# Twelve raw fp32 expert units: the first layer as three products of halves, the second layer left raw

## The chip, the cores and the metric

One NeuronCore of a Trainium2 chip runs the whole kernel. The metric is device time in microseconds (us) of one execution. Names of engines: PE is TensorE (PEld its weight loads), ACT is ScalarE, DVE is VectorE, POOL is GpSimd, SP is the queue that issues most transfers.

## The reference, cut to what matters

A gated linear recurrence runs over four sequences of 3648 tokens with 256 channels. Its output, 14592 rows of 256, goes through a two-level mixture of experts: the largest of 4 group logits and the largest of 4 expert logits inside that group pick one of 16 experts for each token, and that expert's two-layer network is scaled by the product of the two softmax weights.

```python
a_t  = exp(8 * sigmoid(r_gate) * log(sigmoid(a_param)))
h    = a_t[:, t] * h + sqrt(1 - a_t**2)[:, t] * sigmoid(i_gate)[:, t] * x[:, t]   # over t
...
g = argmax(y @ w_group);  e = argmax(y @ w_expert[g])          # per token
out = softmax weights * ( relu(y @ w1[g, e]) @ w2[g, e] )      # w1: 256 x 1024, w2: 1024 x 256
```

## The kernel before, in words

The tokens go through the recurrence in 16 chunks: chunk 0 has 4 blocks of 128 tokens, chunks 1 to 13 have 8, the last two have 4 and 2. For each chunk SP loads `a`, `i` and `x` (two halves each), ACT does the tanh, exp, square and sqrt passes, DVE the products and the scan (L374). PE then turns two blocks at a time into rows (`rows1`, L381, "rows" below) and ACT copies them out of PSUM (`rows2`, L387). DVE computes the routing, PE ranks the tokens (L463, L464), and POOL scatters the rows to lists, one list for each expert, in DRAM (`scatter`, L484, one indirect transfer for each block).

The expert work runs in units of 256 tokens of one expert. A unit takes its rows from the list (`gather`), turns them on PE (four transposes, L1006 for the raw units), and multiplies by `w1` in four steps j = 0 to 3 (first layer), each followed by a relu on ACT and by step j of the second layer with `w2`, one step behind. At the end ACT and DVE scale the two halves of the result (`finish`, L969 and L971) and POOL sends them to the output (`give`, L977).

There are three kinds of expert work, in this order on PE:

- Eight blocks of 128 tokens for four resident experts (`Block`, L1061 and L1073), whose raw fp32 weights lie in four places, k = 0 to 3. Each place is two tiles, one for `w1` and one for `w2`: `w1h0`,`w1l0` / `w2h0`,`w2l0` / `w1h1`,`w1l1` / `w2h1`,`w2l1`.
- Units 0 to 11 (`NATIVE = 12`), which multiply in raw fp32: `w1` is `m.w[0]`, `w2` is `m.w[1]`, the rows `m.x`. Unit u uses place u mod 4. These are `mm1_native` (L1016) and `mm2_native` (L1030).
- From unit 12 on, the units split weights, rows and relu results into two halves in `float32r` (a high half, and a low half that is the difference) and take three products, high by high, high by low, low by high (L886 and L951). Each unit uses all four tiles of b = u mod 2. Units from 26 on need the table that is made after the last chunk; the tail units (three blocks, L886 with 384 columns) end the kernel.

A planner (`Plan`) runs when the kernel is built. Every operation has an engine, an estimated cost, a due time, what it must follow and which buffers it takes, and the planner writes out one fixed order for each engine. Each engine executes its own order and waits where data or a buffer is not there. `STEPN` is the spacing of the due times of the twelve raw units. Buffers that matter here: one `q_o` (the second layer's result in PSUM), one `q_y` (rows, ranks, counts and the small row tables in PSUM), two `q_h` and two `hs` (before and after the relu), two `g` (gathered rows), three `o` (results on their way out).

The expert table of a stage comes from `counts` (L623), 24 small DVE operations and `in_row1` (L670); units 8 to 16 wait for the second such table.

Of the kernel before, what the change touches and what calls it, by code (L numbers as in the profile page):

```python
# [8 lines left out]
F32 = mybir.dt.float32  # L9
F32R = mybir.dt.float32r  # L10
# [35 lines left out]
class Plan:  # L46
# [14 lines left out]
    def op(self, engine, cost, emit, due, after=(), new=(), use=(), dma=0, table=None, soon=0.0, order=()):  # L61
        o = Op(engine, cost, emit, due, new, use, dma, table, soon)
        after = dict.fromkeys(a for a in after if a)
        order = dict.fromkeys(a for a in order if a and a not in after)
        o.wait = len(after) + len(order)
        for b in o.new + o.use:
            b.left += 1
        for a in after:
            a.then.append(o)
        for a in order:  # L70
            a.next.append(o)
        self.ops.append(o)
        return o
# [79 lines left out]
def rglru_moe_kernel(ctx: ExitStack, tc: tile.TileContext, x, r_gate, i_gate, a_param,  # L153
                     w_group, w_expert, w1, w2, out):
    nc = tc.nc
    V, S, G, T, DMA = nc.vector, nc.scalar, nc.gpsimd, nc.tensor, nc.sync

    P, NB = 128, 4
    D, NTOK = x.shape
    SEQ = NTOK // NB  # L160
    NT = NTOK // P
    NE = 16
# [14 lines left out]
    RES, RSTAGES = (0, 4, 8, 12), (1, 2)  # L177
    STAGES = [(4, 8), (7, 9), (10, 9)]
    NATIVE = 12

    BUFS = dict(i=4, x=4, a=8, v=4, wf=6, g=2, xs=2, hs=2, o=3, cl=4)
    PBUFS = dict(q_r=2, q_y=1, q_h=2, q_o=1)
# [11 lines left out]
    ROUTE = OROWS + 12  # L194
    AHEAD = 8

    STEP2, STEPB, STEPN = 10.5, 7.2, 14.5
    FIRST = range(1, 5)
    URGENT = (0, 1, 2, 3, 4, 7)
    ORES = 60  # L200
# [11 lines left out]
            rings[n] = Ring(k)  # L212
            pools[n] = ctx.enter_context(tc.tile_pool(name="p_" + n, bufs=k, **kw))
    rings["gb"] = Ring(NR)
    rings["raw"] = Ring(NR)
    for n in ("d", "oe", "bs", "pi"):
        rings[n] = Ring(2)

    def buf(n):
        return Buf(rings[n])  # L220
# [574 lines left out]
    class Unit:  # L795
        def __init__(self, u, tb, t, due):
            self.u, self.b, self.tb, self.t, self.due = u, u % 2, tb, t, due
            self.nb = 3 if tb is tT else 2
            self.hh, self.hl, self.qo, self.wf, self.cnd, self.c3 = {}, {}, [None] * 3, {}, {}, {}
            self.native = u < NATIVE and tb in tAs  # L800
            self.always = tb is tT or t < 2 or u < NATIVE + 2

        def col(self, what, h):
# [176 lines left out]
        tc.add_to_no_dep_group("out", ins.ins)  # L980


    def raw_places(k):
        b, half = divmod(k, 2)
        names = (("w1h", "w1l"), ("w2h", "w2l"))[half]
        return [wp.tile([P, 2, F] if half == 0 else [P, NF, D], F32, name=f"{n}{b}").rearrange("p a b -> p (a b)")
                for n in names]

    raw = [raw_places(k) for k in range(NR)]

# [4 lines left out]
    def load_native(m, i):  # L995
        if i == 0:
            m.w = raw_places(m.u % NR)
            e = m.reg("ei", [ENG.SP], NE - 1)
            m.src = [t_[bass.ds(e, 1)].rearrange("o p n -> (o p) n") for t_ in (w1, w2)]
        DMA.dma_start(m.w[i], m.src[i])  # L1000

    def turn_native(m):
        m.qx = pools["q_r"].tile([P, 512], F32, name="q_r")
# [83 lines left out]
    def add_blocks(s, ck, rows, masked, scattered):  # L1087
        bs = [Block(s, k, ck.due + ORES + k * STEPB) for k in range(NR)]
        for m in bs:
            due = m.due  # L1090
            bg, bx, q, bc = buf("gb"), buf("xs"), buf("q_r"), buf("cl")
            ga = op("SP", 0.1, lambda m=m: rows_block(m), ck.due + 20, [rows] + scattered, [bg], dma=P * DW * 4)
            tr = op("PE", 0.22, lambda m=m: turn_block(m), due - PREP, [ga], [q], [bg], order=trs[-1:])
            oc = op("DVE", 0.32, lambda m=m: cols_block(m), due - PREP, [tr, masked], [bc], [bg], order=ocs[-1:])
            ocs.append(oc)
            cp = op("ACT", 0.38, lambda m=m: copy_block(m), due - PREP, [tr], [bx], [q], order=cps[-1:])
            trs.append(tr)
            cps.append(cp)
            bo = buf("q_o")
            m1, rl, bh = [], [], []  # L1100
            for j in range(2):
                q = buf("q_h")
                m1.append(op("PE", 1.87, lambda m=m, j=j: mm1_block(m, j), due + j * 1.8, [cp, ld_raw[m.k][0]] + seq[-1:], [q], [bx, raw_b[m.k]]))
                seq.append(m1[-1])
                bh.append(buf("hs"))
                rl.append(op("ACT", 0.6, lambda m=m, j=j: relu_block(m, j), due + j * 1.8 - HASTE, [m1[j]], [bh[j]], [q]))
            for j in range(2):
                seq.append(op("PE", 1.82, lambda m=m, j=j: mm2_block(m, j), due + 3.5 + j * 1.8, [rl[j], ld_raw[m.k][1]] + seq[-1:],
                              [bo] if j == 0 else [], [bh[j], raw_b[m.k]] + ([bo] if j else [])))
            b = buf("o")  # L1110
            f_ = op("DVE", 0.48, lambda m=m: finish_block(m), due, seq[-1:] + [oc], [b], [bo, bc])
            op("POOL", 1.1, lambda m=m: give_block(m), due + STEPB, [f_], use=[b, bc], dma=P * D * 4)
# [12 lines left out]
    def add_native(m, before):  # L1125
        due = m.due
        early = due - WAHEAD
        B = 0.2155
        bw = buf("raw")
        ws = []  # L1130
        for i in range(2):
            ws.append(op("SP", 0.1, lambda i=i: load_native(m, i), early + i * 4, [m.tb.row], [bw] if i == 0 else [],
                         [bw] if i else [], dma=2 * P * F * 4, order=m.lw[-1:]))
            m.lw.append(ws[-1])
        bg, m.bc = buf("g"), buf("cl")
        ga = op("SP", 0.1, lambda: gather(m), early, [m.tb.row] + m.tb.scs, [bg], dma=2 * P * DW * 4, order=gas[-1:])
        gas.append(ga)
        bx, q = buf("xs"), buf("q_r")
        tr = op("PE", 0.107 * 4, lambda: turn_native(m), due - PREP, [ga] + trs[-1:], [q], [bg])
        trs.append(tr)  # L1140
        m.oc = op("DVE", 0.34, lambda: columns(m), due - PREP, [tr], [m.bc], [bg], order=ocs[-1:])
        ocs.append(m.oc)
        cp = op("ACT", 0.6, lambda: copy_native(m), due - PREP, [tr], [bx], [q], order=cps[-1:])
        cps.append(cp)

        def second(j):
            m.p2.append(op("PE", 8 * B, lambda j=j: mm2_native(m, j), due + (j + 1) * STEPN / J,
                           seq[-1:] + [rl[j], ws[1]], [bo] if j == 0 else [], [bh[j], bw] + ([bo] if j else [])))
            seq.append(m.p2[-1])
            if j == J - 1:  # L1150
                add_results(m, [bo], due + STEPN)
        m.p1, m.p2 = [], []
        pend = getattr(before, "pend", None)
        rl, qh, bh = [], {}, {}
        bo = buf("q_o")
        for j in range(J):
            q, bh[j] = buf("q_h"), buf("hs")

            def p1(j=j):
                qh[j] = mm1_native(m, j)  # L1160
            mm = op("PE", 8 * B, p1, due + j * STEPN / J, [cp, ws[0]] + seq[-1:], [q], [bx, bw])
            rl.append(op("ACT", 0.6, lambda j=j: relu_native(m, j, qh[j]), due + j * STEPN / J - HASTE, [mm], [bh[j]], [q]))
            m.p1.append(mm)
            seq.append(mm)
            if pend:
                pend()
            pend = lambda j=j: second(j)
        m.pend = pend
# [78 lines left out]
    def add_counts(gen, costs, due, after, n, more=False, ck=None):  # L1247
        q = buf("q_y")
        cn = op("PE", 0.1, counts, due, after, [q])
        if ck:  # L1250
# [4 lines left out]
    raw_b = [buf("raw") for _ in RES]  # L1255
    ld_raw = [[op("SP", 0.06, lambda k=k, i=i: load_raw(k, i), 40 + k * 9 + 4.5 * i, dma=2 * P * F * 4, soon=32 + k * 9,
                  new=raw_b[k:k + 1] if i == 0 else [], use=raw_b[k:k + 1] if i else []) for i in range(2)] for k in range(NR)]
    seq, gas, trs, cps, ocs = [], [], [], [], []
    ACTWF = []
    scs, eA, res = [], None, []  # L1260
# [24 lines left out]
    for u, m in enumerate(us):  # L1285
        m.lw = chain_lw
        m.lent = []
        if m.native:
            add_native(m, us[u - 1] if u else None)
            continue  # L1290
        if u < NATIVE + 2:
            m.lent = [o for n in us[:NATIVE] if n.u % NR // 2 == m.b for o in n.p1 + n.p2]
        add_unit(m, us[u - 1] if u else None, us[u - 2] if u > 1 else None)
    m.pend()
    cks[0].routed.wait += 1
# [73 lines left out]
```

## Time and profile before

| | us |
|---|---|
| median of 3 runs (range) | 928.49 (927.67 to 932.93) |
| profiled execution, its own time | 938.17 |
| its span in the trace | 936.4 |
| PE busy in the span | 854.5 (91%) |
| first raw unit's first product | 151.27 |
| first product of unit 12 | 376.5 |

The profile's rows give a line of the kernel, the engine, the operation, and what it writes and reads. A raw fp32 product leaves two matmul records, a product of halves one. Matmuls overlap, so the mean time of one record is longer than the distance from one to the next; the distance is read from the chain, where a group of products stands with the time it adds.

### The profile page before, as it was taken

How to read it: one execution, taken by the hardware profiler on the slowest of the kernel's cores; microseconds unless marked ns; L12 is line 12 of the kernel's file. 1: busy time of each engine (PE TensorE's matmuls, PEld its weight loads, DVE VectorE, ACT ScalarE, POOL GpSimd, SP SyncE). 2: the span in 40 equal slices, each digit the busy share in tenths (PEclk: the TensorE clock that was granted, in tenths of full speed). 3: DMA queues.
4: the chain of work that ended last, by engine and by line, in shares of the span. 5: the costliest groups of instructions: out<-in, count | busy, mean ns of one | idle time of the engine just before them, and what ended most of it. 6: DMA issues, size and time to landing. Idle time of an engine off the chain costs nothing.

```text
span 936.4 us, 18547 instructions
## 1 busy us (share of the span) xinstructions
PE 854.5 (91%) x6082; PEld 817.0 (87%) x6082; DVE 624.3 (67%) x1308; ACT 584.7 (62%) x877; POOL 297.7 (32%) x290
## 2 busy tenths in 40 slices
PE   1449899989989999999999999999999999999985
PEld 1338899878868888999999999999999999999985
DVE  5797788778645224787777777777766667566662
ACT  8997889989945233656555555555645455454541
POOL 2256745743852545221111111111121213112132
PEclk9969999999999999999999999999999999999998
DMA  9979879998954636677777767787764556455410
GB/s 302 418 265 399 333 269 416 415 334 315 337 156 152 225 99 210 219 228 243 207 227 226 229 224 226 224 251 250 230 225 128 187 175 213 156 157 169 130 48 22
DMA packets 72733, 216.26 MB, mean 231 GB/s; under 512 B 10517, under 2 KB 28703, under 8 KB 68512
## 3 DMA queue, kind: packets, MB, share of 16 engines
q1 hardware_dynamic: 60736, 183.61, 58.9%
q0 software_dynamic: 11872, 31.10, 8.7%
q8 instruction: 65, 1.06, 0.5%
q14 instruction: 60, 0.49, 0.2%
HBM read 182.76 MB, written 34.00 MB: 231 GB/s over the span
## 4 chain that ended last, share of the span: by engine, by line
PE 70%; issue 4%; DVE 1%; ACT 1%; POOL 1%; another core or an unknown queue 0%; DVEq 0%; POOLq 0%; ACTq 0%
PE q_h L886 26%; PE q_o L951 23%; PE q_o L1030 7%; PE q_h L1016 6%; PE q_y L381 3%; PE q_y L951 3%; PE q_r L862 2%; POOL out_dram L977 1%; PE q_r L1006 0%; ACT o L969 0%; DVE i L893 0%; DVE w2l L841 0%; PE q_y L670 0%; DVE o L973 0%
## 5 line engine op out<-in xcount | busy, mean ns | idle before, releaser
L977 POOL DMA_INDIRECT out_dram<-o,cl x122 | 133.7, 1095 | 454.1 <-ACT o L969 263.4
L484 POOL DMA_INDIRECT y_s<-wf,pi x114 | 142.2, 1247 | 86.0 <-issue 54.9
L886 PE MATMUL q_h<-x,w1h 128*128 128x384 f32 (+1 forms) x512 | 116.0, 315 | 7.5 <-DVE i L893 7.5
L890 ACT ACTIVATE hh<-q_h 128x512 fp32r<-128x512 f32 x100 | 60.3, 603 | 93.8 <-PE q_h L886 77.9
L890 ACT ACTIVATE a<-q_h 128x384 fp32r<-128x384 f32 (+1 forms) x128 | 56.4, 446 | 99.0 <-PE q_h L886 86.5
L886 PE MATMUL q_h<-xh,w1h 128*128 128x256 f32 x400 | 112.9, 282 | 0.0
L886 PE MATMUL q_h<-xl,w1h 128*128 128x256 f32 x400 | 112.7, 282 | 0.0
L886 PE MATMUL q_h<-xh,w1l 128*128 128x256 f32 x400 | 112.6, 281 | 0.0
L893 DVE SCALAR_TENSOR_TENSOR i<-q_h,a 128x384 fp32r<-128x384 f32 (+1 forms) x128 | 60.9, 496 | 74.7 <-ACT a L890 72.5
L841 DVE TENSOR_TENSOR w1l<-wf,w1h 128x1024 fp32r<-128x1024 f32 x82 | 99.9, 1221 | 10.1 <-ACT w1h L839 9.3
L893 DVE SCALAR_TENSOR_TENSOR hl<-q_h,hh 128x512 fp32r<-128x512 f32 x100 | 68.8, 688 | 50.9 <-ACT hh L890 50.9
L841 DVE TENSOR_TENSOR w2l<-wf,w2h 128x1024 fp32r<-128x1024 f32 x82 | 98.2, 1218 | 1.9 <-ACT w2h L839 1.9
L381 PE MATMUL q_y<-yw,a 128*128 128x148 f32 x368 | 60.0, 308 | 35.9 <-DVE a L374 26.2
L886 PEld LDWEIGHTS q_h<-x,w1h 128*128 128x128 f32 x512 | 84.2, 188 | 8.9 <-issue 6.2
L381 PEld LDWEIGHTS q_y<-yw,a 128*128 128x128 f32 x368 | 54.9, 203 | 41.0 <-issue 21.2
L839 ACT CAST w1h<-wf 128x1024 fp32r<-128x1024 f32 x82 | 87.0, 1064 | 0.2 <-issue 0.2
L839 ACT CAST w2h<-wf 128x1024 fp32r<-128x1024 f32 x82 | 83.9, 1043 | 0.0
L886 PE MATMUL q_h<-x,w1l 128*128 128x384 f32 (+1 forms) x256 | 79.8, 312 | 0.0
L886 PEld LDWEIGHTS q_h<-xh,w1h 128*128 128x128 f32 x400 | 75.4, 188 | 0.1
L886 PEld LDWEIGHTS q_h<-xh,w1l 128*128 128x128 f32 x400 | 75.3, 188 | 0.0
L886 PEld LDWEIGHTS q_h<-xl,w1h 128*128 128x128 f32 x400 | 75.2, 188 | 0.0
L971 DVE TENSOR_SCALAR o<-q_o,cl 128x256 f32<-128x256 f32 x53 | 25.6, 484 | 63.1 <-ACT o L969 30.4
(342 smaller groups left out, 1975.1 us busy)
## 6 DMA issues: line engine op xcount, KB each, us to landing
wf<-in_moe_w_dram SPq DMA_DIRECT2D x164, 512.0 KB
a<-in_r_gate_dram SPq DMA_DIRECT2D x26, 512.0 KB
i<-in_i_gate_dram SPq DMA_DIRECT2D x26, 512.0 KB
x<-in_x_dram SPq DMA_DIRECT2D x26, 512.0 KB
g<-y_s SPq DMA_DIRECT2D x37, 276.0 KB
w1h<-in_moe_w_dram SPq DMA_DIRECT2D x8, 1024.0 KB
w1l<-in_moe_w_dram SPq DMA_DIRECT2D x8, 1024.0 KB
w2h<-in_moe_w_dram SPq DMA_DIRECT2D x8, 1024.0 KB
```

Source lines behind the costliest of these rows:

```text
L381: T.matmul(q[:, k, h * P:h * P + YW], lhsT=ck.t["a", h][:, (2 * i + k) * P:(2 * i + k + 1) * P], rhs=yw[:, h, :], start=h == 0, stop=h == ...
L484: ins = G.indirect_dma_start(out=y_s, out_offset=bass.IndirectOffsetOnAxis(ap=ck.pi[:, k:k + 1], axis=0), in_=ck.t["yo", k // 4][:, k % 4, ...
L839: S.copy(hi[m.b][:, sl], src)
L841: V.tensor_tensor(lo[m.b][:, sl], src, hi[m.b][:, sl].bitcast(F32), op=ALU.subtract)
L886: T.matmul(q, lhsT=w[m.b][:, c, fs], rhs=mv[:, c, :N], start=n == 0, stop=n == 5)
L890: S.activation(hh, q, AF.Relu)
L893: V.scalar_tensor_tensor(hl, q, 0.0, hh.bitcast(F32), op0=ALU.max, op1=ALU.subtract)
L951: T.matmul(m.qo[h], lhsT=mv, rhs=w[m.b][:, 2 * j + f, :], start=j == f == n == 0, stop=(j, f, n) == (J - 1, 1, 2))
L971: V.tensor_scalar(o, m.qo[h], m.col("cw", h), None, op0=ALU.mult)
L977: ins = G.indirect_dma_start(out=out, out_offset=bass.IndirectOffsetOnAxis(ap=m.col("idx", h), axis=0), in_=m.o[h], in_offset=None, bounds ...
L1016: T.matmul(q[:, f * TS:(f + 1) * TS], lhsT=m.w[0][:, c * F + (2 * j + f) * P:c * F + (2 * j + f + 1) * P], rhs=m.x[:, c * TS:(c + 1) * TS] ...
L1030: T.matmul(m.qo[h], lhsT=m.hh[j][:, f * TS + h * P:f * TS + (h + 1) * P], rhs=m.w[1][:, (2 * j + f) * D:(2 * j + f + 1) * D], start=j == f ...
```

## The change

For units 0 to 11 the first layer is computed as in the later units: `w1` and the gathered rows are each split into a high and a low `float32r` half, and each raw product becomes three. The second layer, `w2` and the relu result stay raw fp32.

- Each unit now takes the four tiles of b = u mod 2. Raw `w1` is loaded in two parts of 512 KB into `w2l`, ACT copies each part to `w1h` (high half) and DVE writes the difference to `w1l`; raw `w2` is loaded into `w2h`. Before, unit u used one pair of tiles out of four pairs; now out of two sets of four.
- The copy of the turned rows by ACT stays one operation, now to the high half; one DVE subtraction is added for the low half.
- Step j of the first layer is 12 products of halves where it was 4 raw products. The planner's cost for it is 12 x 0.1195 where it was 8 x 0.2155, and `STEPN` is 13.4 where it was 14.5.
- Units 12 and 13, which take over the tiles, now wait for the raw units of the same b, and places of the resident experts are freed tile by tile.

```diff
-    STEP2, STEPB, STEPN = 10.5, 7.2, 14.5
+    STEP2, STEPB, STEPN = 10.5, 7.2, 13.4
...
+    def load_halves(m, i, k):
...
+        if k == 0:
+            m.w[i] = one_place(f"w2{'lh'[i]}{m.b}")
+        sl = slice(k * F, (k + 1) * F) if i == 0 else slice(0, 2 * F)
+        DMA.dma_start(m.w[i][:, sl], m.src[i][:, sl])
+
+    def split_halves(m, k, part):
+        if k == 0:
+            m.w["hl"[part]] = one_place(f"w1{'hl'[part]}{m.b}", F32R)
+        sl = slice(k * F, (k + 1) * F)
+        if part == 0:
+            S.copy(m.w["h"][:, sl], m.w[0][:, sl])
+        else:
+            V.tensor_tensor(m.w["l"][:, sl], m.w[0][:, sl], m.w["h"][:, sl].bitcast(F32), op=ALU.subtract)
+
+    def copy_halves(m):
+        m.xh = pools["xs"].tile([P, 2 * TS], F32R, name="xh")
+        S.copy(m.xh, m.qx)
+
+    def rest_halves(m):
+        m.xl = pools["xs"].tile([P, 2 * TS], F32R, name="xl")
+        V.tensor_tensor(m.xl, m.qx, m.xh.bitcast(F32), op=ALU.subtract)
+
+    def mm1_halves(m, j):
+        q = m.qh = pools["q_h"].tile([P, 512], F32, name="q_h")
+        for f in range(2):
+            n = 0
+            for c in range(2):
+                at = c * F + (2 * j + f) * P
+                for w, mv in (("h", m.xh), ("h", m.xl), ("l", m.xh)):
+                    T.matmul(q[:, f * TS:(f + 1) * TS], lhsT=m.w[w][:, at:at + P], rhs=mv[:, c * TS:(c + 1) * TS],
+                             start=n == 0, stop=n == 5)
+                    n += 1
+        return q
...
+        if m.halves:
+            b1, b2, bs_ = [buf(f"w1h{m.b}"), buf(f"w1l{m.b}")], [buf(f"w2h{m.b}")], buf(f"w2l{m.b}")
+            for k in range(2):
+                lw = fetch(0.1, lambda k=k: load_halves(m, 0, k), early + 2 * k, [] if k else [bs_], [bs_] if k else [], P * F * 4)
+                his.append(op("ACT", 1.05, lambda k=k: split_halves(m, k, 0), due - PREP + 3 * k, [lw], [] if k else b1[:1],
+                              [bs_] + (b1[:1] if k else []), order=his[-1:]))
+                ws.append(op("DVE", 1.22, lambda k=k: split_halves(m, k, 1), due - PREP + 3 * k, [his[-1]], [] if k else b1[1:],
+                             [bs_, b1[0]] + (b1[1:] if k else [])))
+            w2_ = [fetch(0.1, lambda: load_halves(m, 1, 0), early + 6, b2, [], 2 * P * F * 4)]
...
-            mm = op("PE", 8 * B, p1, due + j * STEPN / J, [cp, ws[0]] + seq[-1:], [q], [bx, bw])
+            mm = op("PE", 12 * 0.1195 if m.halves else 8 * B, p1, due + j * STEPN / J, [cp] + ws + seq[-1:], [q], [bx] + b1)
...
-            m.lent = [o for n in us[:NATIVE] if n.u % NR // 2 == m.b for o in n.p1 + n.p2]
+            m.lent = [o for n in us[:NATIVE] if (n.b if n.halves else n.u % NR // 2) == m.b for o in n.p1 + n.p2]
```

The planner writes a new order from the first raw unit to about unit 15; before and after that the orders of all engines agree but for line numbers. Three places matter below.

First place: SP where it loads the weights of unit 0. Before, row 98 (`w1h`) and row 100 (`w1l`) are raw `w1` and `w2` in place 0, and unit 1 follows in place 1:

```order
L1000 DMA w1h_1300<-in_moe_w_dram 128x2048
L1000 ISA
L1000 DMA w1l_1301<-in_moe_w_dram 128x2048
L262 DMA x<-in_x_dram 128x1024
L262 DMA i<-in_i_gate_dram 128x1024
```

After, `w2l` takes raw `w1` in two parts and `w2h` raw `w2`:

```order
L265 DMA x<-in_x_dram 128x1024
L265 DMA i<-in_i_gate_dram 128x1024
L811 TENSOR_LOAD sm_1241
L811 ISA x2
L1017 ISA
L1017 DMA w2l_1378<-in_moe_w_dram 128x1024
L1017 ISA
L1017 DMA w2l_1378<-in_moe_w_dram 128x1024
L1017 ISA
L1017 DMA w2h_1381<-in_moe_w_dram 128x2048
```

Two chunk loads (`x`, `i`) moved ahead of the unit's weights, and the tile that is filled first is now one that resident block 1 reads last.

Second place: ACT around the second expert table (the one that units 8 to 16 wait for), where it copies rows from `q_y` (L387 before, L390 after). Before:

```order
L1022 ACTIVATE hh<-q_h 128x512
L969 ACTIVATE o<-q_o,cl 128x256
L334 ACT_TABLE_LOAD
L334 ACTIVATE a<-a 128x1024
L387 COPY wf<-q_y 128x552
```

After:

```order
L1068 ACTIVATE hh<-q_h 128x512
L342 ACTIVATE a<-a,la 128x1024
L337 ACTIVATE a<-a 128x1024
L350 ACTIVATE v<-a 128x1024
L390 COPY wf<-q_y 128x552
```

The copy stands behind other chunk work than before; on PE, the table's matmul (L670 before, L673 after) comes 0.4 us of transposes behind the rows that this copy empties before, and one step of each layer behind them after.

Third place: POOL, where two chunks' scatters (L484 before, L487 after) stand together. Before, between the results of unit 2 and of unit 3:

```order
L977 DMA out_dram<-o,cl 14592x256 x2
L391 IOTA wf 128x4 x2
L484 DMA y_s<-wf,pi 241920x276 x16
L977 DMA out_dram<-o,cl 14592x256 x2
L391 IOTA wf 128x4
```

After, between the results of unit 9 and of unit 10:

```order
L981 DMA out_dram<-o,cl 14592x256 x2
L487 DMA y_s<-wf,pi 241920x276 x16
L394 IOTA wf 128x4
L981 DMA out_dram<-o,cl 14592x256 x2
L394 IOTA wf 128x4
```

The run of 16 scatters moved from the fourth unit to the eleventh; between them chunks and results now alternate.

More of the change, by code (lines that the diff above doesn't have):

```diff
@@ L179, in rglru_moe_kernel @@
     NATIVE = 12
+    HALVES = range(0, NATIVE)
     BUFS = dict(i=4, x=4, a=8, v=4, wf=6, g=2, xs=2, hs=2, o=3, cl=4)
@@ L214, in rglru_moe_kernel @@
     rings["gb"] = Ring(NR)
-    rings["raw"] = Ring(NR)
+    for b in range(2):
+        for n in ("w1h", "w1l", "w2h", "w2l"):
+            rings[f"{n}{b}"] = Ring(1)
     for n in ("d", "oe", "bs", "pi"):
@@ L800, in __init__ @@
             self.native = u < NATIVE and tb in tAs
+            self.halves = self.native and u in HALVES
             self.always = tb is tT or t < 2 or u < NATIVE + 2
@@ L980, in give, with one_place, raw_names @@
         tc.add_to_no_dep_group("out", ins.ins)
+    def one_place(name, dtype=F32):
+        return wp.tile([P, 2, F] if name < "w2" else [P, NF, D], dtype, name=name).rearrange("p a b -> p (a b)")
+    def raw_names(k):
+        return [f"{n}{k // 2}" for n in (("w1h", "w1l"), ("w2h", "w2l"))[k % 2]]
     def raw_places(k):
[L984 to L987, printed above, removed]
+        return [one_place(n) for n in raw_names(k)]
     raw = [raw_places(k) for k in range(NR)]
@@ L1000, in load_native @@
         DMA.dma_start(m.w[i], m.src[i])
+    def load_halves(m, i, k):
+        if (i, k) == (0, 0):
+            m.w = {}
+            e = m.reg("ei", [ENG.SP], NE - 1)
+            m.src = [t_[bass.ds(e, 1)].rearrange("o p n -> (o p) n") for t_ in (w1, w2)]
+        if k == 0:
[27 more added lines that the diff above has]
+        return q
     def turn_native(m):
@@ L1102, in add_blocks @@
                 q = buf("q_h")
-                m1.append(op("PE", 1.87, lambda m=m, j=j: mm1_block(m, j), due + j * 1.8, [cp, ld_raw[m.k][0]] + seq[-1:], [q], [bx, raw_b[m.k]]))
+                m1.append(op("PE", 1.87, lambda m=m, j=j: mm1_block(m, j), due + j * 1.8, [cp, ld_raw[m.k][0]] + seq[-1:], [q], [bx, raw_b[m.k][0]]))
                 seq.append(m1[-1])
@@ L1108, in add_blocks @@
                 seq.append(op("PE", 1.82, lambda m=m, j=j: mm2_block(m, j), due + 3.5 + j * 1.8, [rl[j], ld_raw[m.k][1]] + seq[-1:],
-                              [bo] if j == 0 else [], [bh[j], raw_b[m.k]] + ([bo] if j else [])))
+                              [bo] if j == 0 else [], [bh[j], raw_b[m.k][1]] + ([bo] if j else [])))
             b = buf("o")
@@ L1128, in add_native, with fetch @@
         B = 0.2155
[L1129 to L1134, printed above, removed]
+        ws, his = [], []
+        def fetch(cost, go, at, new, use, dma):
+            o = op("SP", cost, go, at, [m.tb.row], new, use, dma=dma, order=m.lw[-1:])
+            m.lw.append(o)
+            return o
+        if m.halves:
[7 more added lines that the diff above has]
+            w2_ = [fetch(0.1, lambda: load_halves(m, 1, 0), early + 6, b2, [], 2 * P * F * 4)]
+        else:
+            b1, b2 = ([buf(n)] for n in raw_names(m.u % NR))
+            ws.append(fetch(0.1, lambda: load_native(m, 0), early, b1 + b2, [], 2 * P * F * 4))
+            w2_ = [fetch(0.1, lambda: load_native(m, 1), early + 4, [], b2, 2 * P * F * 4)]
         bg, m.bc = buf("g"), buf("cl")
@@ L1142, in add_native @@
         ocs.append(m.oc)
-        cp = op("ACT", 0.6, lambda: copy_native(m), due - PREP, [tr], [bx], [q], order=cps[-1:])
+        cp = op("ACT", 0.6, lambda: (copy_halves if m.halves else copy_native)(m), due - PREP, [tr], [bx], [q], order=cps[-1:])
         cps.append(cp)
+        if m.halves:
+            ws.append(op("DVE", 0.69, lambda: rest_halves(m), due - PREP, [cp], (), [q, bx]))
         def second(j):
             m.p2.append(op("PE", 8 * B, lambda j=j: mm2_native(m, j), due + (j + 1) * STEPN / J,
-                           seq[-1:] + [rl[j], ws[1]], [bo] if j == 0 else [], [bh[j], bw] + ([bo] if j else [])))
+                           seq[-1:] + [rl[j]] + w2_, [bo] if j == 0 else [], [bh[j]] + b2 + ([bo] if j else [])))
             seq.append(m.p2[-1])
@@ L1159, in p1 @@
             def p1(j=j):
-                qh[j] = mm1_native(m, j)
-            mm = op("PE", 8 * B, p1, due + j * STEPN / J, [cp, ws[0]] + seq[-1:], [q], [bx, bw])
+                qh[j] = (mm1_halves if m.halves else mm1_native)(m, j)
+            mm = op("PE", 12 * 0.1195 if m.halves else 8 * B, p1, due + j * STEPN / J, [cp] + ws + seq[-1:], [q], [bx] + b1)
             rl.append(op("ACT", 0.6, lambda j=j: relu_native(m, j, qh[j]), due + j * STEPN / J - HASTE, [mm], [bh[j]], [q]))
@@ L1253, in add_counts @@
         return chain(gen, costs[n:], due, [o], more=more)[1] if n < len(costs) else o
-    raw_b = [buf("raw") for _ in RES]
+    raw_b = [[buf(n) for n in raw_names(k)] for k in range(NR)]
     ld_raw = [[op("SP", 0.06, lambda k=k, i=i: load_raw(k, i), 40 + k * 9 + 4.5 * i, dma=2 * P * F * 4, soon=32 + k * 9,
-                  new=raw_b[k:k + 1] if i == 0 else [], use=raw_b[k:k + 1] if i else []) for i in range(2)] for k in range(NR)]
+                  new=raw_b[k][i:i + 1]) for i in range(2)] for k in range(NR)]
     seq, gas, trs, cps, ocs = [], [], [], [], []
```

## The prediction

> **What bounds the kernel now.** I read the page first: which engine is busy, how that runs over the span, and what the chain that ended last consists of.
>
> ```profile
> PE 854.5 (91%) x6082; PEld 817.0 (87%) x6082; DVE 624.3 (67%) x1308; ACT 584.7 (62%) x877; POOL 297.7 (32%) x290
> PE   1449899989989999999999999999999999999985
> ACT  8997889989945233656555555555645455454541
> PE 70%; issue 4%; DVE 1%; ACT 1%; POOL 1%; another core or an unknown queue 0%; DVEq 0%; POOLq 0%; ACTq 0%
> PE q_h L886 26%; PE q_o L951 23%; PE q_o L1030 7%; PE q_h L1016 6%; PE q_y L381 3%; PE q_y L951 3%; PE q_r L862 2%; POOL out_dram L977 1%; PE q_r L1006 0%; ACT o L969 0%; DVE i L893 0%; DVE w2l L841 0%; PE q_y L670 0%; DVE o L973 0%
> ```
>
> 70% of the span is PE work on the chain, and L1016, the line that changes, is 6% of it. ACT is close to full only in the first dozen slices. Next the stretches of the raw units, and the units behind them.
>
> ```profile
> core 0: us, PE busy (x) PEld busy (x) DVE busy (x) ACT busy (x) POOL busy (x), PEclk, DMA share, GB/s
> 151.00:200.00 49.00, 46.82 (x248) 41.36 (x247) 34.80 (x100) 44.85 (x56) 37.14 (x32) 0.97 1.01 410
> 200.00:260.00 60.00, 55.26 (x309) 49.41 (x309) 46.59 (x87) 56.57 (x76) 29.00 (x28) 1.00 0.86 306
> 260.00:320.00 60.00, 57.10 (x285) 49.42 (x285) 28.34 (x120) 25.14 (x45) 24.14 (x29) 0.95 0.50 162
> 320.00:376.00 56.00, 54.09 (x270) 47.10 (x269) 17.02 (x70) 16.93 (x30) 26.47 (x29) 1.00 0.53 173
> 376.00:676.00 300.00, 300.00 (x2525) 299.08 (x2524) 224.01 (x378) 178.24 (x280) 53.94 (x52) 1.00 0.74 231
> ```
>
> From 376 us on PE has no gap for 300 us. So whatever is won before unit 12 starts is kept, as long as nothing behind waits for chunks: the table of units 26 and later comes from the last chunk, and those units start some 160 us later (14 units of eight 1.43 us steps). The question is when unit 12 starts. From 151 to 376, PE is busy 213.3 of 225 us. ACT and the DMA engines are nearly full up to 260 (56.57 of 60 us; 1.01 and 0.86), and both half empty afterwards. Three waits make up 8 of the 11.7 us that PE is idle:
>
> ```profile
> PE q_o L1030 <- issue: 3.4, 1, 3.4
> PE q_o L1030 <- DVE o L971: 2.4, 1, 2.4
> PE q_y L670 <- issue: 2.2, 1, 2.2
> ```
>
> **The change part by part.** *First-layer products.* The chain gives the distances, raw steps first, then a step of halves, then two raw steps that followed an idle stretch:
>
> ```profile
> 284.70 1.73 PE q_h L1016 x8
> 376.71 1.43 PE q_h L886 x12
> 259.63 3.68 PE q_o L1030 x8
> 280.01 3.60 PE q_o L1030 x8
> ...
> L1016 PE MATMUL q_h<-xh,w1h x192: 379/379/608, 151.3 to 359.8; 128*128 128x256 f32 x192
> L1016 PE MATMUL q_h<-xh,w2h x192: 379/379/462, 166.9 to 374.1; 128*128 128x256 f32 x192
> ```
>
> 384 records at 8 for a step are 48 steps, four in each of 12 units. A step falls from 1.73 to 1.43 us: 48 x 0.30 = **14.4 us** less on PE, all on the path. The second layer keeps its 1.73.
>
> The Trainium skill, "FP8 and Floating Point Precision", section TensorE Precision Notes, says that true fp32 takes four passes through the array. By that alone a step of halves is three quarters of a raw one, an estimate of 1.30 us, and the term would be 20.8 us. The trace has 1.43 for it, so 14.4 stands.
>
> *Splitting.* The rows of the later units have the same operations on the same shapes; the last is a subtraction out of PSUM over 512 columns:
>
> ```profile
> L839 ACT CAST w1h<-wf x82: 1039/1065/1078, 350.2 to 899.9; 128x1024 fp32r<-128x1024 f32 x82
> L841 DVE TENSOR_TENSOR w1l<-wf,w1h x82: 1212/1222/1227, 351.2 to 901.3; 128x1024 fp32r<-128x1024 f32 x82
> L893 DVE SCALAR_TENSOR_TENSOR hl<-q_h,hh x100: 670/692/693, 378.9 to 673.8; 128x512 fp32r<-128x512 f32 x100
> ```
>
> ACT gets 24 x 1.065 = 25.6 us, DVE 24 x 1.222 + 12 x 0.692 = 37.6. Over the whole stretch, shortened to some 211 us, ACT comes to 143.5 + 25.6 = 169 (80%) and DVE to 126.8 + 37.6 = 164 (78%), so both have room. They have none before 260: there the splits push chunk work back, by 2.13 us of ACT for each unit. What covers that is the distance between a chunk's scan and its rows on PE. For chunk 10, where it is smallest as I read the order:
>
> ```profile
> 205.64 2.35 DVE L374 TENSOR_TENSOR_SCAN a<-a,v 128x1024 f32<-128x1024 f32 x1
> ...
> 233.08 1.17 PE L381 MATMUL q_y<-yw,a 128*128 128x148 f32 x8
> ```
>
> The scan ends at 208.0, its rows come at 233.1: 25 us. Five units' splits take 10.7 of them. The cost on the path is zero while that cover holds; each microsecond beyond it is a microsecond of PE.
>
> *Loads.* Same bytes, 36 issues in place of 24, but SP executes in order, and the tiles come free later. Unit 0's raw `w1` now goes to the tile that resident block 1 reads last, unit 1's to that of block 3:
>
> ```profile
> 129.89 3.62 PE L1073 MATMUL q_o<-w2l,hh 128*128 128x256 f32 x16
> 133.54 0.34 SPq L1000 DMA_DIRECT2D w2l<-in_moe_w_dram x1
> ...
> 149.46 1.97 PE L1073 MATMUL q_o<-w2l,hh 128*128 128x256 f32 x8
> 151.47 0.33 SPq L1000 DMA_DIRECT2D w2l<-in_moe_w_dram x1
> ...
> 151.27 1.89 PE L1016 MATMUL q_h<-xh,w1h 128*128 128x256 f32 x8
> ```
>
> Unit 0's parts are issued at about 133.6, 17.7 us before its first product; a megabyte at 410 GB/s is 2.6 us and the splits 3.4 (two casts, one more subtraction), so 151.3 stays. Unit 1's are issued at 151.5, about 15 us before its first product. Behind each of them chunk loads and gathers wait on SP. I put the DMA time lost at 2 to 4 us for each of these two waits, 6 in all, which again comes out of the 25 us. From unit 2 on, raw `w2` waits on SP for the last second-layer step two units before; it is needed some 16 us later. Units 12 and 13 take their tiles from units 10 and 11, one unit later than unit 12 did; that leaves the rest of unit 11, some 10 us, for two casts and a subtraction.
>
> *Waits that go.* The 2.2 us at L670 is ACT: the single `q_y` was emptied late, behind a table load and a tanh.
>
> ```profile
> 192.21 1.06 ACT L334 ACTIVATE a<-a 128x1024 f32<-128x1024 f32 x1
> 193.18 0.60 ACT L387 COPY wf<-q_y 128x552 f32<-128x552 f32 x1
> ...
> 193.83 1.02 PE L670 MATMUL q_y<-yw,t 128*1 128x128 f32 x6 [2.18 <-issue]
> ```
>
> In the new order a step of each layer, 1.43 + 1.73 = 3.2 us, stands between rows and table instead of 0.4 of transposes, so this wait should go. With it goes what follows an idle stretch of over 2 us: the first raw step then takes 3.60 to 3.68 in place of 1.73, so 1.9 more. Together **-3.9** (2.18 + 1.7, the clock being half for a little less than that step).
>
> The Trainium skill, "TensorE: Matmul & The Clock Gate", section What's actually happening, puts the return to half clock after an idle window of about 3.4 us. By that a gap of 2.2 would cost only itself and this term would be -2.2. The trace disagrees: after 2.4 us idle the step at 280.01 took 3.60.
>
> *The run of 16 scatters.* The 3.4 us wait comes from it: POOL was late with results, the three `o` were full, and the single `q_o` was not emptied.
>
> ```profile
> 254.57 2.13 POOL L977 DMA_INDIRECT out_dram<-o,cl x1 [0.30 <-issue]
> ...
> 259.10 0.48 DVE L971 TENSOR_SCALAR o<-q_o,cl 128x256 f32<-128x256 f32 x1 [3.18 <-DMA out_dram<-o,cl]
> ```
>
> It moves to unit 10, where the DMA share is 0.5; I keep its cost, zero net.
>
> *Waits that come.* ACT and DVE are now dense over the whole stretch, and PE waits on ACT for `q_y`, for the relu (3.2 us of cover, before 3.5) and for `finish`. Nearest rows: 376 to 676, with ACT at 59% and DVE at 75%, has 0.00 us idle; 200 to 260, with ACT at 94%, has 4.74 in 60, which over 211 us would be 16.7, 5 above today's 11.7, and two more half-clock steps make it 8.6. ACT at 80% lies between; I take **+4**.
>
> Sum: -14.4 - 3.9 + 4 = -14.3. The profiled execution takes 938.17 (span 936.4, 1.8 around it), 9.7 above the median; its sum gives 923.9. The same step from the median of 928.5 gives **914**.
>
> **The rivals.** *More of the waits go*: the three above and their half-clock steps are 8.0 + 3 x 1.8 = 13.4; if they go and none come, 928.5 - 14.4 - 13.4 = 901. For it: the run of scatters moves to an emptier place. Against: the fixed order misjudges some copies in any arrangement, as these three show. The quicker step of 1.30 us ends near here too (914 - 6.4 = 908), and the rows of the later units speak against it.
>
> *The gain is eaten*: PE waits for late copies, relus and finishes cost about +16, so 926.5. That needs six more gaps of 1 us and five of them long enough for a half-clock step of 1.9. For it: ACT at 94% already lost 4.74 us in 60. Against: before, relus held PE for 0.3 us in all.
>
> *Slower: SP's order starves the chunks.* The wait for `w2` two units back holds the chunk loads behind it. If each of units 2 to 5 costs 5 us of DMA time, chunk 10 is late by 6 + 20 + 10.7 = 37, 12 more than the cover; PE waits 12 us in about three gaps, 1.9 more each: 928.5 - 14.4 + 17.7 = 932. It decides from 25 us of lateness on and passes the gain at 25 + 14. For it: DMA share 1.01 up to 200, so lost time is not made up there. Against: from 260 on the share is 0.50, and the later chunks have more cover.
>
> **How the numbers follow.** Forecast (906 to 921) 0.60, more waits gone (898 to 906) 0.13, eaten (921 to 930) 0.16, slower (above 930) 0.11. The range 902 to 930 leaves out the slower case and most of the best one's lower half, about 2 in 10. This kernel's runs can tell about 0.5%, 4.6 us: faster is below 923.9, slower above 933.1. Faster takes the first two and a little of the third, 0.77; slower the upper part of the last, 0.08; the same 0.15.
>
> **What would show it.** In the profile after: a step of the first layer at 1.43 us in the chain; unit 12's first product about 14 us earlier, near 362; ACT and DVE near 80% up to there; no idle time before L673; chunk scans 10 to 20 us later, and rows (L384) that don't wait for them. Wrong would be: rows waiting for a scan, first-layer steps waiting for `w1l`, several PE gaps above 2 us with the clock halved behind them, or unit 0 starting later than 152.

## The result, and the profile after

| us | before | after |
|---|---|---|
| median, runs side by side (range) | 931.75 (927.67 to 933.84) | **915.24** (913.38 to 917.9) |
| ratio of the runs, 95% interval | | **0.984** (0.9816 to 0.9864) |
| profiled execution, its own time | 938.17 | 913.47 |
| unit 0's first product | 151.3 | 151.5 |
| from there to unit 12's first product | 225.2 | 192.6 |
| from there to the end of PE's last product | 548.4 | 556.1 |

The kernel is 16.5 us faster by the medians. The three lower rows are read off PE's timeline. They say that more was won before unit 12 than was forecast (32.6 us, where about 14 were foreseen), and that 7.7 us of it were given back behind.

The page after: busy time of each engine, and PE and ACT in 40 slices.

```profile
PE 835.7 (92%) x6274; PEld 811.8 (89%) x6274; DVE 655.8 (72%) x1344; ACT 607.6 (67%) x901; POOL 304.1 (33%) x290
PE   1349899999999998999999999999999999999984
ACT  8997979999999734566656555655555454555541
```

ACT now stays full up to slice 13, before up to slice 11; PE has one slice below 9 in the middle, the sixteenth. By stretches (columns as in the prediction's table; the last two rows are the place where time is given back):

```profile
151.00:200.00 49.00, 49.00 (x336) 45.91 (x336) 39.53 (x108) 46.16 (x59) 34.94 (x31) 1.00 0.94 362
200.00:260.00 60.00, 59.82 (x404) 56.39 (x403) 52.72 (x102) 57.61 (x75) 31.78 (x30) 1.00 0.89 318
260.00:320.00 60.00, 60.00 (x411) 56.26 (x410) 49.25 (x142) 51.28 (x78) 31.37 (x31) 1.00 0.67 228
344.00:360.00 16.00, 13.52 (x109) 12.98 (x107) 11.29 (x44) 7.95 (x14) 8.28 (x10) 0.98 0.75 245
360.00:368.00 8.00, 7.13 (x38) 6.84 (x39) 6.74 (x20) 2.35 (x4) 3.37 (x3) 0.61 0.79 265
```

Up to 320 PE is idle for 0.18 us where it was idle for 9.8, at full clock, with ACT at 96% of 200 to 260. All of PE's waits from 140 to 376:

```profile
PE q_h L890 <- DVE w1l L845: 3.4, 2, 3.1
PE q_o L1119 <- ACT wf L390: 1.1, 1, 1.1
PE q_y L384 <- ACT wf L390: 0.2, 1, 0.2
```

The three large waits of before (table, full `o`, results) are all gone, and the large one that came is not in the changed units. Products in PE's timeline, the second and the last of a first-layer step of one of units 0 to 11, and what follows:

```profile
209.22 0.28 PE L1043 MATMUL q_h<-xl,w1h 128*128 128x256 f32 x1
...
210.41 0.28 PE L1043 MATMUL q_h<-xh,w1l 128*128 128x256 f32 x1
210.53 1.17 PE L384 MATMUL q_y<-yw,a 128*128 128x148 f32 x8
```

Eleven products start from 209.22 on and before 210.53, 0.119 us each; twelve make the forecast step of 1.43.

The wait that came, in the timelines of PE, DVE and SP:

```profile
357.24 0.28 PE L890 MATMUL q_h<-xl,w1h 128*128 128x256 f32 x1
360.67 0.58 PE L890 MATMUL q_h<-xh,w1l 128*128 128x256 f32 x1 [3.15 <-DVE w1l L845]
363.54 1.05 PE L955 MATMUL q_o<-w2h,hh 128*128 128x256 f32 x4
...
367.56 0.64 PE L955 MATMUL q_o<-w2h,hh 128*128 128x256 f32 x4
...
348.70 0.42 DVE L437 TENSOR_TENSOR_SCAN inc<-smask,oe 128x128 f32<-128x128 f32 x1
359.30 0.17 DVE L618 TENSOR_SCALAR t<-t 128x16 int32<-128x16 int32 x1
359.39 1.22 DVE L845 TENSOR_TENSOR w1l<-wf,w1h 128x1024 fp32r<-128x1024 f32 x1
...
345.18 12.74 SPq L827 DMA_DIRECT2D wf<-in_moe_w_dram  x5
```

What SP waited for from 318 to 372 (us in total, times, longest), the first line:

```profile
SPq L827 <- DMA y_s<-wf,pi: 20.1, 4, 9.1
```

This is unit 13: unit 12 began at 344.11 and its four relus are done at 355.3. (The expectations below call it unit 14.) SP issues weight loads of the split units from 345.18 on and needs 12.74 us for five, because the six `wf` tiles serve both these weights and the rows of the chunks, and POOL is still scattering the last chunks' rows out of them (20.1 us of SP's waits are for scatters; the longest, 9.1, lies in this row). Then DVE does the last chunk's routing (L437 is one of its steps) and the last table (L618) before the subtraction that PE waits for. Behind the gap PE runs at half clock for a while: the group of four products at 363.54 takes 1.05, the next of the kind 0.64. The clock column has 0.61 over 8 us and 0.98 over 16, which is 3.4 us lost; with 3.35 of gaps that makes, as an estimate, 6.8 of the 7.7.

### The profile page after: what moved, and what is told of

It reads as the page before. It is cut to its first block, busy times and chain, and to the rows that moved or that the text cites. A ratio compares the mean times of both kernels' runs of the same rounds, so it can differ in the third digit from the quotient of the medians.

```text
span 911.7 us, 19039 instructions
## 1 busy us (share of the span) xinstructions
PE 835.7 (92%) x6274; PEld 811.8 (89%) x6274; DVE 655.8 (72%) x1344; ACT 607.6 (67%) x901; POOL 304.1 (33%) x290
## 5 line engine op out<-in xcount | busy, mean ns | idle before, releaser
L981 POOL DMA_INDIRECT out_dram<-o,cl x122 | 137.3, 1126 | 469.1 <-ACT o L973 290.8
L487 POOL DMA_INDIRECT y_s<-wf,pi x114 | 143.0, 1254 | 75.5 <-issue 61.0
L845 DVE TENSOR_TENSOR w1l<-wf,w1h 128x1024 fp32r<-128x1024 f32 x82 | 100.0, 1221 | 10.6 <-ACT w1h L843 10.2
L1076 PE MATMUL q_o<-w2h,hh 128*128 128x256 f32 x384 | 91.3, 380 | 0.0
L384 PE MATMUL q_y<-yw,a 128*128 128x148 f32 x368 | 59.5, 306 | 33.9 <-DVE a L377 25.6
L1076 PEld LDWEIGHTS q_o<-w2h,hh 128*128 128x128 f32 x384 | 69.5, 190 | 7.5
```

Of the source, the lines that this page charges most:

```text
L384: T.matmul(q[:, k, h * P:h * P + YW], lhsT=ck.t["a", h][:, (2 * i + k) * P:(2 * i + k + 1) * P], rhs=yw[:, h, :], start=h == 0, stop=h == ...
L487: ins = G.indirect_dma_start(out=y_s, out_offset=bass.IndirectOffsetOnAxis(ap=ck.pi[:, k:k + 1], axis=0), in_=ck.t["yo", k // 4][:, k % 4, ...
L845: V.tensor_tensor(lo[m.b][:, sl], src, hi[m.b][:, sl].bitcast(F32), op=ALU.subtract)
L981: ins = G.indirect_dma_start(out=out, out_offset=bass.IndirectOffsetOnAxis(ap=m.col("idx", h), axis=0), in_=m.o[h], in_offset=None, bounds ...
L1076: T.matmul(m.qo[h], lhsT=m.hh[j][:, f * TS + h * P:f * TS + (h + 1) * P], rhs=m.w[1][:, (2 * j + f) * D:(2 * j + f + 1) * D], start=j == f ...
```

## The experiments

Each set of four ran on one chip beside the kernel before. In the first set the kernel before took 944.4 us, some 14 us more than in the others, so times are compared inside a set only. "First" is unit 0's first product, "stretch" from there to unit 12's, "rest" from there to the end of PE's last product; these are of one profiled execution each.

| run | set | median | ratio to before (95%) | first | stretch | rest |
|---|---|---|---|---|---|---|
| before, again | 1 | 946.96 (one time) | | 150.8 | 234.2 | 548.5 |
| order alone | 1 | 943.67 | 0.9994 (0.9974 to 1.0013) | 151.9 | 227.9 | 548.4 |
| six units | 1 | 941.67 | 0.9974 (0.9951 to 0.9998) | 151.0 | 216.4 | 559.1 |
| two products | 1 | 937.33 | 0.9931 (0.9901 to 0.9961) | 150.1 | 222.2 | 557.5 |
| after, again | 2 | 914.67 | 0.9841 (0.9821 to 0.9861) | 150.5 | 194.3 | 556.3 |
| loads early | 2 | 915.69 | 0.9838 (0.9822 to 0.9854) | 151.8 | 194.7 | 556.5 |
| seven `wf` | 2 | 912.6 | 0.9819 (0.9802 to 0.9835) | 149.0 | 197.9 | 551.2 |
| distance 14.5 | 2 | 922.33 | 0.992 (0.9901 to 0.994) | 151.2 | 209.5 | 548.4 |
| raw price | 3 | 927.64 | 0.9977 (0.9961 to 0.9992) | 151.7 | 206.4 | 556.6 |
| split twice | 3 | 933.65 | 1.0038 (1.002 to 1.0056) | 154.5 | 211.3 | 556.6 |
| distance alone | 3 | 937.55 | 1.0093 (1.0075 to 1.011) | 149.5 | 210.6 | 561.1 |
| before, third | 3 | 927.73 (one time) | | 150.1 | 215.9 | 548.4 |

The median of before was 930.57 in the second set and 929.72 in the third. The theory was that the gain is the cheaper products on a full PE, with some waits gone by the new order and some time given back behind. The main rival was that the order, the rings (two sets of four weight tiles in place of four pairs) and the planned distance make the gain, and a second one that the waits of before belong to its one profiled execution.

**Is the first profile of before typical?** No edit.

> The kernel before once more, for a second profile. It tells whether the 20 us that PE loses between unit 0's first product and unit 12's (11.7 us of gaps and three half-clock stretches) belong to the kernel or to the one profiled execution. Theory (they belong to the kernel, since the order on each engine is fixed): unit 12's first product again 222 to 228 us after unit 0's, with gaps above 2 us at the table of the routing and at a full set of o tiles. Rival (they were partly of that execution, which was 6 us above the median): 212 to 219 us, with one or two of the three gaps above 2 us missing.

> The kernel before, a third profile. All profiles of raw units so far agree within 1 us outside the stretch from unit 0 to unit 12, so the median of 930 would leave it 217 to 218 us. Theory (the first profile, 938, had some 8 us of waits more than is usual): 214 to 221 us, with gaps at the table and at the results of 1 to 3 us. Rival (the kernel's usual stretch is 225): 223 to 228.

The waits of the third profile, from 151 us on:

```profile
PE q_o L1030 <- DVE o L971: 4.3, 1, 4.3
PE q_y L670 <- ACT wf L387: 2.2, 1, 2.2
PE q_y L381 <- ACT wf L387: 0.7, 1, 0.7
```

The places are those of the first profile, so they belong to the kernel. Their number and length do not: outside the stretch the three profiles agree within 1.2 us, inside they read 225.2, 234.2 and 215.9. The third has the time that is nearest to the usual median, so the first profile had some 9 us of loss more than is usual. What makes these waits longer in one execution, or on the chip of the first set, no run shows; one scatter took 1.25 us on POOL and one copy of rows 0.62 on ACT in all three.

**The new rings and order without the split.**

```diff
-    HALVES = range(0, NATIVE)
+    HALVES = range(0, 0)
...
-    STEP2, STEPB, STEPN = 10.5, 7.2, 13.4
+    STEP2, STEPB, STEPN = 10.5, 7.2, 14.5
```

> The changed kernel with no unit split: the raw fp32 products, their loads and the unit spacing of 14.5 are as before, and only the weight tiles are rings of their own as in the changed kernel. Theory (the cheaper products are what the change is worth, 14.4 us, and the order some us beside it): 924 to 934, unit 12's first product 215 to 228 us after unit 0's, steps of 1.73. Rival (the new rings or the new order remove the waits by themselves): 914 to 921, unit 12's first product below 212 us after unit 0's.

The ratio is 0.9994, no change: the rings by themselves give nothing. The absolute numbers expected do not fit this set.

**Half the units.**

```diff
-    HALVES = range(0, NATIVE)
+    HALVES = range(0, 6)
```

> Units 0 to 5 split their first layer as in the changed kernel, units 6 to 11 stay raw. Theory (24 of 48 steps are cheaper by 0.30 us, and waits go as far as the order is eased before unit 6): 7.2 us of products and some 3 to 5 us of waits, 917 to 923. The 7 us that the changed kernel gives back at unit 14 stay or shrink, since unit 12 starts later and the last chunk's work has more time. Rival (the gain is from the order, all or nothing): like the changed kernel, 913 to 917, or like the one before, 928 to 933.

Its ratio of 0.9974 stands between the others, but it is less than half of the change. The stretch is 17.8 us shorter than that of before in this set, and the rest 10.6 longer: the give-back did not shrink, it grew. (The planned distance is 13.4 in this run, for the raw units too.) That part of the expectation was wrong.

**One product less.**

```diff
-                for w, mv in (("h", m.xh), ("h", m.xl), ("l", m.xh)):
+                for w, mv in (("h", m.xh), ("l", m.xh)):
...
```

> The changed kernel without the product of w1's high half and the rows' low half: two products in place of three in each first-layer step of the twelve units (part of the result is left out); the order is the same. 48 steps lose 0.48 us, 22.9 us in all. Theory (PE is full up to unit 12 and everything taken from it counts there, but the last chunk's work, which ends at a time of its own, gives it back at units 13 and 14): unit 12's first product 18 to 23 us earlier than 344, but a total of 908 to 915, since the waits behind it grow from 7 us to 15 or more. Rival 1 (nothing behind waits more): 890 to 896. Rival 2 (ACT and DVE are already the bound before unit 12): unit 12's first product less than 10 us earlier, with PE gaps at rows, relus or results, total 905 to 915.

22.9 us less of products than in the changed kernel, yet only 0.7% below before. Waits from 151 to 372, the longest ones:

```profile
PE q_o L1076 <- DVE o L975: 6.3, 3, 4.4
PE q_y L673 <- ACT wf L390: 5.1, 1, 5.1
PE q_y L466 <- ACT wf L390: 3.9, 1, 3.9
PE q_o L1076 <- ACT hh L1068: 3.8, 3, 3.0
```

The waits stand before unit 12, as the second rival had it; those behind hardly grew (a rest of 557.5). How much of them is this chip's and how much the order's stays open, since the changed kernel did not run in this set.

**The changed kernel again.** No edit.

> The changed kernel once more, beside the others of this set. In the set before, the kernel before lost 26 us from unit 0 to unit 12 where its first profile had 20. Theory (the lost time before unit 12 comes from places of the order, which the changed kernel does not have): again 190 to 198 us from unit 0 to unit 12, 550 to 557 us from unit 12 to the last product, time 1.5 to 3% below the kernel before. Rival (the empty gaps were luck of one profiled execution, and the changed kernel loses time at the same kind of places as soon as transfers are a little slower): 200 to 215 us from unit 0 to unit 12, time less than 1% below.

As the theory had it: stretch, rest and ratio all repeat.

**What holds unit 13.** Loads due 35 us ahead of a unit (loads early), or one `wf` tile more and one `v` tile (an input of the chunks' scans) less (seven `wf`), each by itself.

```diff
-    HASTE, SPLIT, PREP, WAHEAD = 8, 8, 12, 25
+    HASTE, SPLIT, PREP, WAHEAD = 8, 8, 12, 35
...
-    BUFS = dict(i=4, x=4, a=8, v=4, wf=6, g=2, xs=2, hs=2, o=3, cl=4)
+    BUFS = dict(i=4, x=4, a=8, v=3, wf=7, g=2, xs=2, hs=2, o=3, cl=4)
```

> The changed kernel with every unit's loads due 35 instead of 25 us ahead. Theory (units 13 and 14 wait because their weights' loads stand on SP behind the wf tiles of the last chunks' rows, and then on DVE behind the last chunk's routing): loads due 10 us earlier are in the order ahead of those rows, the gap of 3.2 us and the half clock behind it go, and unit 12 to the end takes 549 to 551 in place of 556; 5 to 7 us less in all, unless earlier loads hold up the chunks before. Rival (the wf tiles are the limit in any order, since rows and weights share six): 0 to 2 us less, or some us more.

> The changed kernel with seven wf tiles in place of six, and three v tiles in place of four to make room. Theory (the wf tiles hold the weights of units 13 and 14): unit 12 to the end 549 to 553 us; if three v tiles hold back the chunks' normalisation, unit 12 itself comes 3 to 8 us later, so 3 us less to 5 more in all. Rival (DVE's order alone holds unit 14): unit 12 to the end stays 555 to 557.

SP's timeline at that place, with earlier due times and then with seven tiles, where the wait on PE that is left follows:

```profile
347.56 12.90 SPq L827 DMA_DIRECT2D wf<-in_moe_w_dram  x5
```

```profile
347.85 3.38 SPq L827 DMA_DIRECT2D wf<-in_moe_w_dram  x4
...
378.43 0.58 PE L890 MATMUL q_h<-xh,w1l 128*128 128x256 f32 x1 [1.65 <-DVE w1l L845]
```

With earlier due times SP's row and the wait are as in the changed kernel; with seven tiles four loads go out in 3.4 us. So it is not the due time that holds the loads but, as far as these two runs show, the tiles. The planner makes a new order with seven tiles as well, in which the last chunk's routing begins 11.3 us ahead of unit 12 (335.65 against 346.92); the runs do not tell tiles and order apart. The rest falls from 556.3 to 551.2, 5.1 of the 7.9 us; a shorter wait for `w1l` is left one unit later. The stretch is 3.6 longer, with two waits of 1.3 and 1.5 us for rows' copies that the changed kernel lacks. By the medians it is the fastest version, 2.1 us below the changed kernel, but their intervals overlap.

**The planned distance.** `STEPN` 14.5 with split units (distance 14.5), and 13.4 with raw units (distance alone).

```diff
-    STEP2, STEPB, STEPN = 10.5, 7.2, 13.4
+    STEP2, STEPB, STEPN = 10.5, 7.2, 14.5
...
-    HALVES = range(0, NATIVE)
+    HALVES = range(0, 0)
```

> The changed kernel with the planned distance of two units at 14.5 us, as it was before the change; the work is the same. Theory (the planned distance only shifts chunk work against units by up to 13 us at unit 12, and gives the last chunk's work more time ahead of unit 14): unit 0 to unit 12 within 4 us of the changed kernel, unit 12 to the end 549 to 554, in all 1 to 6 us less. Rival (the smaller distance is what removed the waits before unit 12): 8 us or more later at unit 12, and 4 us or more in all.

> No unit split, as in the run of the order alone, but with the planned distance of 13.4 us. With the run at 14.5 of raw units and the two of split units this makes a square of four. Theory (the distance is worth its 8 us only together with the shorter units, since raw units need over 14 us each on PE): within 4 us of the kernel before, 927 to 934. Rival (the distance alone is worth 8 us, whatever the products): 919 to 925.

| ratio to before | distance 14.5 | distance 13.4 |
|---|---|---|
| raw units | 0.9994 (set 1) | 1.0093 (set 3) |
| split units | 0.992 (set 2) | 0.9841 (set 2) |

The two act together. The shorter distance costs raw units 0.9% and gains split units 0.8%. Both expectations missed half of it: I had held 14.5 for harmless or better with split units. With split units at 14.5, the largest wait in PE's timeline, its cause on DVE, and POOL where the two results stand between scatters:

```profile
337.88 3.58 PE L1076 MATMUL q_o<-w2h,hh 128*128 128x256 f32 x8 [6.62 <-DVE o L975]
...
337.34 0.48 DVE L975 TENSOR_SCALAR o<-q_o,cl 128x256 f32<-128x256 f32 x1 [4.64 <-DMA out_dram<-o,cl]
...
328.50 0.98 POOL L487 DMA_INDIRECT y_s<-wf,pi  x1 [0.31 <-issue]
329.79 0.98 POOL L981 DMA_INDIRECT out_dram<-o,cl  x1 [0.30 <-ACT wf L390]
331.08 0.98 POOL L981 DMA_INDIRECT out_dram<-o,cl  x1 [0.31 <-issue]
332.37 1.09 POOL L487 DMA_INDIRECT y_s<-wf,pi  x1 [0.30 <-issue]
```

It is the wait of before: two results behind a long run of scatters on POOL, `o` full, `q_o` not emptied. With raw units at 13.4 the stretch is 5.3 us shorter than in the third profile of before, and the rest 12.7 longer: a wait of 4.79 us for `w1h`, whose cast waits for its load, stands at unit 14. In these four, the longer distance leaves waits ahead of unit 12 and the shorter one waits behind it: every run planned at 14.5 has a rest of 548.4 or 548.5, every one at 13.4 with six `wf` tiles one of 556 to 561.

**The products' price, with order, loads and splits left alone.**

```diff
+                more = c == 0 or (j % 2 == 1 and f == 0)
-                for w, mv in (("h", m.xh), ("h", m.xl), ("l", m.xh)):
+                for w, mv in (("h", m.xh), ("h", m.xl), ("l", m.xh)) + (("l", m.xl),) * more:
...
```

> The changed kernel with the fourth product, low half by low half, added for five of the eight sums of two steps: 14 or 15 matmuls in a first-layer step in place of 12, so that a step takes about 1.73 us again, the raw price; order, loads and splits are those of the changed kernel. Added PE work 48 x 2.5 x 0.119 = 14.3 us. Theory (PE is full from unit 0 to unit 12 in this order, so each microsecond of product counts there; later units then give less back at unit 14, since the last chunk's work has more time): unit 0 to unit 12 207 to 210 us in place of 194, unit 12 to the end 548 to 554 in place of 556, in all 8 to 14 us more, 922 to 929. Rival (PE has hidden room, what the products cost is not what the change is worth): unit 0 to unit 12 below 201, in all less than 5 us more.

14.3 us of PE work cost 13.0 us by the medians (927.64 against 914.67, each with before within 1 us of the other). The stretch grows by 12 to 14 us; the rest stays at 556.6, against the expectation that it would shrink. Unit 12 starts 14.0 us later than in the changed kernel (358.10 against 344.11), but the last chunk's routing is 14.0 later too, and the wait behind it is as long as it was:

```profile
362.70 0.42 DVE L437 TENSOR_TENSOR_SCAN inc<-smask,oe 128x128 f32<-128x128 f32 x1
374.52 0.39 PE L890 MATMUL q_h<-xh,w1l 128*128 128x256 f32 x1 [3.00 <-DVE w1l L845]
```

The orders of the engines are those of the changed kernel, so the last chunk's work moved together with the units. This is the test that separates theory and rival: at the raw price the changed kernel is 0.2% faster than before. The price makes about 13 of the gain, all else that the change does about 2. That holds for this order: in the table of four above, split units are 0.7% faster than raw ones at 14.5, and 2.5% at 13.4.

**The splits twice.**

```diff
-        if part == 0:
-            S.copy(m.w["h"][:, sl], m.w[0][:, sl])
+        for _ in range(2):
+            if part == 0:
+                S.copy(m.w["h"][:, sl], m.w[0][:, sl])
...
```

> The changed kernel with each cast to a high half and each subtraction to a low half of w1 in the twelve units made twice: 25.6 us more on ACT and 29.3 on DVE, with the order unchanged. Theory (the splits are hidden by the distance of a chunk's scan and its rows, 25 us, of which the change has used 18 to 20): five units' second splits push chunk 10 by another 10.7 us, some 5 more than is left, and PE waits about that in two or three gaps: 5 to 10 us more in all, 920 to 925, with waits at the rows or at results. Rival 1 (ACT and DVE have room beyond that): 914 to 917. Rival 2 (ACT is what bounds the stretch): about 25 us more, 935 to 940.

It costs 19.0 us, far more than the 5 to 10 expected; 3 to 4 of them come before unit 0 (154.5). The sum of the stretches from 151 to 320, 169 us, and PE's longest waits from 151 to 400:

```profile
sum 169.00, PE 157.33 PEld 144.58 DVE 151.85 ACT 164.35 POOL 83.34; mean PE 52.44 PEld 48.19 DVE 50.62 ACT 54.78 POOL 27.78
```

```profile
PE q_y L384 <- ACT wf L390: 6.5, 6, 1.7
PE q_h L890 <- DVE w1l L845: 4.4, 2, 4.2
PE q_o L1077 <- DVE o L975: 3.4, 3, 1.8
```

ACT is busy 97%, and 7.5 of the 13.8 us of waits ahead of unit 12 are for its copies of rows. So the first splits were hidden and a second set of the same size is not: of 25.6 us on ACT, 19 come out at the end. My expectation counted only how late a chunk's rows come, with 5 to 7 us of cover left where the changed kernel has 2.0 (next section); it left out that on a full ACT the copy that empties `q_y` stands behind the casts too.

## Why the prediction came out, point by point

- **First-layer products, -14.4: right.** 1.43 a step; put back, they cost 13.0.
- **Splits hidden: right, with almost nothing left.** Chunk 10's scan begins at 225.15 where it began at 205.64, 19.5 later, and of the 25 us of cover 2.0 are left:

```profile
225.15 2.34 DVE L377 TENSOR_TENSOR_SCAN a<-a,v 128x1024 f32<-128x1024 f32 x1
229.45 1.17 PE L384 MATMUL q_y<-yw,a 128*128 128x148 f32 x8
```

The scans of chunks 9 and 11 to 13 are 20 to 32 us later, more than the 10 to 20 foreseen, and chunks 9 to 13 have 1.6 to 4.9 us left. No rows waited for a scan. The second set of splits shows how near the edge this is.

- **Loads: right for unit 0** (151.5 and 150.5; forecast 151.3). The DMA share fell from 1.01 to 0.94 between 151 and 200, some 3.4 us of DMA time where 6 were foreseen for two waits; PE paid nothing for it.
- **Waits that go, -3.9: too few.** Full work at the raw price is 206.4 us (the stretch of the raw-price run, which has no wait inside). Before had 215.9 in its usual kind of execution, so 9.5 us of loss, and 225.2 in the first profile, 18.8. All of it went, not the table's wait alone.
- **The run of 16 scatters, zero net: wrong.** It moved to 321.84 as the order showed, but PE did not wait there. In this profile the two results ahead of it left POOL by 321.5.
- **Waits that come, +4: too few, and misplaced.** Ahead of unit 12 the two profiles of the changed kernel have 0.2 and 1.7 us of gaps; 7.7 and 7.9 us came behind it.
- **The step that failed** is the reading that "whatever is won before unit 12 starts is kept, as long as nothing behind waits for chunks", with its check on the tables of unit 26 on and on the freeing of units 12's and 13's tiles. It left out that those units' weights share `wf` with the chunks' rows, and DVE with the last chunk's routing. In the first pair of profiles unit 12 came 32 us earlier and the last chunk's second scan 20.6 later (311.42 against 290.83). The place in the order counts, not the early start by itself: with split units, unit 12 starts at 360.7 at a distance of 14.5 and at 358.1 in the raw-price run, and the rests are 548.4 and 556.6. The last chunk's routing begins 28.9 us ahead of unit 12 in the one (331.75) and 4.6 behind it in the other, as in the changed kernel; in the first profile of before it is 15.2 ahead (361.27).
- **The signs named.** Unit 12's first product came at 344.1, not near 362. Up to there ACT was busy 85% and DVE 80%, where both were foreseen near 80. One sign of being wrong did appear, a first-layer step that waits for `w1l`, though in unit 13 and not in the twelve.
- **The sum.** Forecast -14.4 - 3.9 + 4. Measured, by the usual median: -13.0 for the price, some -9.5 for waits, +7.8 given back, -14.7 against -15.9 to -16.5 by the medians; the 1 to 2 us between are not assigned. The 914 rests on one right term and on two errors of some 6 and 4 us that nearly cancel, which is luck. Setting the step off from the median, not from the profiled 938, was right: the pair of profiles differs by 24.7 us, the medians by 16.5.

## What to carry to other kernels

When work is cut on a full engine, ask also what everything behind shares with the work alongside: buffers, queues, and the other engines' fixed order. Where that order puts the work alongside decides: dearer products moved it together with the units, another planned distance moved it against them. To price one term of a change that also moves the order, put that cost back and leave the order alone. And take a second profile before counting waits: the places repeat, the sizes may not.

## What the runs showed of the hardware

The half clock does not follow every gap of the same length. A gap of 2.18 us before the table's product is in the first and in the third profile of before; these are the steps behind it, first then third:

```profile
193.83 1.02 PE L670 MATMUL q_y<-yw,t 128*1 128x128 f32 x6 [2.18 <-issue]
194.68 3.40 PE L1030 MATMUL q_o<-w1l,hh 128*128 128x256 f32 x8
```

```profile
192.63 1.02 PE L670 MATMUL q_y<-yw,t 128*1 128x128 f32 x6 [2.18 <-ACT wf L387]
193.48 1.89 PE L1030 MATMUL q_o<-w1l,hh 128*128 128x256 f32 x8
```

3.40 against 1.89 after the same gap, so the prediction's 1.7 for it is no fixed price. In every trace the half-clock stretches begin on a grid of 3.41 us: in the first profile at 109.57, 194.91, 259.76 and 280.24, which are 25, 19 and 6 steps apart. There the gap lies inside one step of the grid, 191.50 to 194.91, in which PE was busy for 1.2 us, and the next step has half the clock. In the third profile a border of the grid, at 191.86, falls into the gap; PE was busy for 2.0 and 2.6 us of the two steps, and the clock stayed full. In all fourteen traces, from 125 to 880 us, each of the 26 steps at full clock in which PE was busy for less than 1.5 us was followed by half clock, and none in which it was busy for more than 2.1. The Trainium skill, "TensorE: Matmul & The Clock Gate", section What's actually happening, speaks of a free-running window of about 3.4 us. The traces agree with a window that runs on its own; that a gap of 2.18 us was ever enough does not agree with a whole window of idleness.
